# Cluster attention and spatial gating: more MLP buffers, weight splitting on other engines, sums on PE, and new plan constants

## The chip, the cores and the metric

One core of a Trainium2 chip runs the whole kernel. The metric is device time in microseconds (us) of one execution; three runs of the kernel before gave a median of 691.05 (690.49 to 691.19). The engines are PE (matrix products; its loading of weights is shown as PEld), DVE (vector), ACT (activation functions and scaled copies), POOL (a further elementwise engine) and SP, whose queue only issues DMA. Each engine works through its own queue in order.

## The reference

Inputs are q, k and v of 4 batches, 8 heads, 768 positions and 64 dimensions, 16 centroids a head, and the weights of an MLP. Cut to its core:

```python
q_assign = argmax(q_n @ c_n)            # nearest centroid, by cosine
k_assign = argmax(k_n @ c_n)
mask   = q_assign[..., :, None] == k_assign[..., None, :]
scores = where(mask, q @ k.T / sqrt(64), -1e9)
attn   = exp(scores - max(scores)); attn /= sum(attn) + 1e-9
x      = attn @ v                       # heads side by side: 768 x 512
h      = relu(x @ w_in)                 # 512 -> 1024
u, v   = h[..., :512], h[..., 512:]
v_n    = (v - mean(v)) / sqrt(var(v) + 1e-6)
v_s    = w_spatial @ v_n + b_spatial    # over the 768 positions
out    = (u * v_s) @ w_out              # 512 -> 512
```

## The kernel before

**Numbers.** Every fp32 operand of a matrix product is held as two fp16 parts: a high part (a scaled copy, usually on ACT) and a low part (what the rounding left, a scaled difference on DVE or a plain difference on POOL). Products are then three: high times high, high times low, low times high.

**Attention.** A step is a pair of heads; there are 16 (four batches of four pairs), numbered n. `prep(n)` loads q and k and v, splits them, finds the nearest centroids with small products (L553 to L555) and a one-hot encoding on DVE (L566 to L578), and writes these rows beside the head's 64 rows, so that a product over 81 rows yields the masked score. It also makes the sum of v over all positions for rows that meet no key, which goes as two more rows into `mean`. For pairs 0 to 3 that sum is twelve fp16 products with a matrix of ones on PE (L613, L614); for pairs 4 to 15 (`short`) it is a reduction of the raw v on DVE (L621) and two small fp32 products (L622). `shifts(n)` computes each row's maximum: products on PE (L662) and maxima on DVE (L669). `attend(n)` goes over two heads and six tiles of 128 keys each: scores on PE (L713, L715), exp on ACT (L719), high part on ACT (L721), low part on POOL (L722), value products on PE (L727). Then DVE divides by the row's sum, and ACT and POOL split the result x (L750, L751), which a transposing DMA brings into `xT`.

**MLP.** `mlp(b)` runs per batch on six tiles of 128 positions, beside the attention of later batches; the last batch's MLP runs when all attention is done. All its long products are line L771. `v_tile` projects and ACT evicts into `v32` (L792, two buffers, `MV_BUFS`); DVE takes mean and variance; two tiles are normalised together (L811), split on DVE and POOL (L812, L813). `u_tile` projects u (L822). `s_tile` makes the spatial product with `wsp`, DVE adds the bias and multiplies by u (L832), DVE and POOL split it (L833, L834), and a transposing DMA brings it into `gT` (two buffers). `p_tile` makes the output product with `wou`, ACT evicts it into `o32` (L842, one buffer), and ACT's queue issues the store (L843).

**Weights.** `weights` loads each piece and splits it in `lows`: high part on ACT (L461), low part on DVE (L462). `w_in` is split early. `w_spatial` (twelve pieces of 128 x 384, raw buffers `wraw`, two of them) and then `w_out` (eight pieces, three more DVE steps each, L477 to L479) come later, at times given by `WL_AT` and `WL_GAP`. Loads go through SP's queue.

**Order.** All of this is written as operations with an engine, a planned duration, what they come after, and a key. `Plan.run` is a list scheduler: it plays the operations against a model of the engines and, for each engine that comes free, emits the ready operation of the smallest key; for operations of attention the key is added to a due time (`due`, from `DUE_0`, `DUE`, `DUE_M`), for others to the time at which they became ready. So a constant or a planned duration changes the order of instructions on every engine, not the instructions. Buffers of a ring are reused in turn, and the hardware waits follow from the data.

Of the kernel before, what the change touches and what calls it, by code (L numbers as in the profile page):

```python
# [7 lines left out]
F32 = mybir.dt.float32  # L8
F16 = mybir.dt.float16
U32 = mybir.dt.uint32  # L10
AF = mybir.ActivationFunctionType
ALU = mybir.AluOpType
AX = mybir.AxisListType
PSUM = bass.MemoryType.PSUM

P = 128

QK_SCALE = 2.0 ** 5
# [19 lines left out]

R_OH, R_SH, R_E, R_END = 64, 80, 81, 83
P32_BUFS = 3  # L40
DUE_0 = 43.04
DUE = 25.06
DUE_PREP = -1.8
DUE_MAX = -0.66
DUE_M = 31.24
DUE_W = 1.2
PT_BUFS = 4
HQ_BUFS = 4
V_BUFS = 2
MV_BUFS = 2  # L50
U_BUFS = 4
MM = 6
W_KEY = 7.7
WL_KEY = 0.91
WL_AT = 183.98
WL_GAP = 3.25
W_AT = 28.34
W_GAP = 5.52
PREP_KEY = 2.81
AV_KEY = 1.09  # L60
K_SC = -2.4
K_MX = -2.81
K_MAX = -0.27

TBL = 0.14
K_SH = -3.11
K_EXP = 0.71
K_HI = -1.78
K_LO = 2.77
K_RC = -1.64  # L70
K_XD = 3.66
K_X = -1.98
K_VT = -3.58
# [63 lines left out]
class Plan:  # L137
# [12 lines left out]
    def op(self, eng, cost, fn, after=(), use=(), new=(), claim=(), key=0.0, at=0.0, dma=None, turn=False, cols=0, alt=None, due=None):  # L150
        o = Op()
        o.due = self.due if due is None else due
        o.eng, o.cost, o.fn, o.key, o.at, o.dma, o.turn, o.cols, o.alt = eng, cost, fn, key, at, dma, turn, cols, alt
        o.after = [a for a in after if a is not None]
        o.new, o.claim, o.order = list(new), list(claim), []
        o.outs, o.end, o.seq = [], None, len(self.ops)
        for t in list(use) + o.new + o.claim:
            t.users.append(o)
        self.ops.append(o)
        return o  # L160
# [115 lines left out]
def kernel(  # L276
# [24 lines left out]
    V, A, T, G_ = nc.vector, nc.scalar, nc.tensor, nc.gpsimd  # L301
# [5 lines left out]
    moe = ctx.enter_context(tc.tile_pool(name="moe", bufs=2))  # L307
# [4 lines left out]
    op = plan.op  # L312
    R = plan.ring
# [54 lines left out]
    r_y = R(sm, "y", [P, 2], F32, 2)  # L368
    r_y2 = R(sm, "y2", [P, 2], F32, 2)
    r_v32 = R(moe, "v32", [P, DF], F32, MV_BUFS)  # L370
    r_o32 = R(moe, "o32", [P, DM], F32, 1)
    r_u32 = R(moe, "u32", [P, DF], F32, U_BUFS)
    r_ghl = R(moe, "ghl", [P, 2, DF], F16, 1)
    r_gT = R(moe, "gT", [P, 2 * NDT, P], F16, 2)
# [28 lines left out]
    def fill():  # L403
# [27 lines left out]
    o = op("PE", 0.3, lambda: T.transpose(out=ct.t[:, 0:P], in_=scratch.t[:, 0:2 * D], identity=idt()), after=[o, ld_i], use=[scratch], new=[ct], key=KC)  # L431
# [20 lines left out]
    def weights(jobs, at, gap, key, raws, tops, on, after=()):  # L452
        ends = []
        for m, (src, dst, n, lg, wide, cell) in enumerate(jobs):
            raw = raws.new()
            sc = 2.0 ** lg
            t0 = at + gap * m

            def lows(x, ld, n=n, dst=dst, sc=sc, raw=raw, cell=cell, use=()):

                h = op("ACT", 0.2 + 0.00085 * n, lambda: A.activation(out=dst()[:, 0, :], in_=x(), func=AF.Copy, scale=sc), after=ld, use=use, key=key)  # L461
                lo = op("DVE", (0.05 if n > 384 else 0.4) + 0.00125 * n, lambda: V.scalar_tensor_tensor(out=dst()[:, 1, :], in0=x(), scalar=sc, in1=dst()[:, 0, :], op0=ALU.mult, op1=ALU.subtract), after=[h], use=use, key=key)  # L462
                w_ops.setdefault(cell, []).extend([h, lo])
                ends.append(lo)

            if not wide:
                ld = move(on, lambda q, raw=raw, src=src, n=n: q.dma_start(out=raw.t[:, :n], in_=src), new=[raw], dma=1.1, at=t0, key=2, after=after)
                lows(lambda raw=raw, n=n: raw.t[:, :n], [ld], use=[raw])
                continue

            top = tops.new()
            ld = move(on, lambda q, raw=raw, src=src, n=n: q.dma_start(out=raw.t[:, :2 * n].bitcast(U32), in_=src.bitcast(U32)), new=[raw], dma=0.0058 * n, at=t0, key=2, after=after)

            def words(raw, n, k):
# [41 lines left out]
    def prep(n):  # L516
        plan.due = due(n, DUE_PREP) if n else None
        b, p = divmod(n, NPR)
        X = pair[n] = {}
        hq, lo, vh, mw = r_hq.new(), r_lo.new(), r_vhl.new(), r_mean.new()  # L520
        X.update(hq=hq, lo=lo, vhl=vh, mean=mw)
        KP = PREP_KEY if n else KP0
        KV = PREP_KEY + 3.0
        raw, vraw = r_raw.new(), r_vraw.new()
# [5 lines left out]
        his, los = [], []  # L530
        for h, ld in enumerate(raws):
            his.append(op("ACT", 0.83, lambda h=h: A.activation(out=hq.t[:, 0, h, :], in_=raw.t[:, h, :], func=AF.Copy, scale=QK_SCALE), after=[ld], use=[raw] + ([hq] if h else []), new=[] if h else [hq], key=KP))  # L532
        for h, ld in enumerate(raws):
            if n == 1:
                o = op("ACT", 0.83, lambda h=h: A.activation(out=raw.t[:, h, :], in_=raw.t[:, h, :], func=AF.Copy, scale=QK_SCALE), after=[his[h]], use=[raw], key=KP)
                los.append(op("POOL", 1.7, lambda h=h: G_.tensor_tensor(out=lo.t[:, h, :], in0=raw.t[:, h, :], in1=hq.t[:, 0, h, :], op=ALU.subtract), after=[o], use=[raw, hq] + ([lo] if h else []), new=[] if h else [lo], key=KP))
                continue
            los.append(op("DVE", 1.4 if n else 0.96, lambda h=h: V.scalar_tensor_tensor(out=lo.t[:, h, :], in0=raw.t[:, h, :], scalar=QK_SCALE, in1=hq.t[:, 0, h, :], op0=ALU.mult, op1=ALU.subtract), after=[his[h]], use=[raw, hq] + ([lo] if h else []), new=[] if h else [lo], key=KP))  # L538
        if n == 0:
            qa0 = [op("ACT", 0.75, lambda x=x: A.copy(out=hq.t[0:D, x], in_=hq.t[D:P, 0]), after=his, use=[hq], key=KP) for x in (1, 2)]  # L540
        else:
            qa0 = [sp(lambda: nc.sync.dma_start(out=hq.t[0:D, 1:3], in_=hq.t[D:P, 0].unsqueeze(1).broadcast_to([D, 2, 2, S])), 1.8, after=his, use=[hq], key=KP)]
        qa1 = sp(lambda: nc.sync.dma_start(out=hq.t[D:P, 2], in_=lo.t[D:P]), 0.9, after=los, use=[hq, lo], key=KP)
# [69 lines left out]
                T.matmul(out=o[:, :, 0:D + 1], lhsT=ones, rhs=vh.t[:, t, :, 0:D + 1], start=(t == 0), stop=False, skip_group_check=True)  # L613
                T.matmul(out=o[:, :, 0:D], lhsT=ones, rhs=vh.t[:, t, :, D + 2:], start=False, stop=(t == NT - 1), skip_group_check=True)  # L614

        short = n >= NPR
        m = D if short else D + 1
        unit = MEAN_UNIT * (V_SCALE if short else 1.0)
        if short:
            vs = r_vs.new()  # L620
            o = op("DVE", 0.9, lambda: V.tensor_reduce(out=vs.t, in_=vraw.t.rearrange("p t c -> p c t"), axis=AX.X, op=ALU.add), after=[ldv], use=[vraw], new=[vs], key=KV)  # L621
            o = op("PE", 0.4, lambda: T.matmul(out=sv.t[0:2, 0:2 * (D + 2)].rearrange("p (h d) -> p h d", h=2)[:, :, 0:D], lhsT=one32, rhs=vs.t.rearrange("p (h d) -> p h d", h=2), start=True, stop=True), after=[o, c_wh], use=[vs], new=[sv], cols=512, key=KV)  # L622
        else:
            o = op("PE", 0.75, sums, after=[o_vh, o_vl, c_wt], use=[vh], new=[sv], cols=1548, key=KV)
# [136 lines left out]
    def mlp(b):  # L761
# [75 lines left out]
        def p_tile(t, tr, pos):  # L837
            gT = gTs[t]
            o32 = r_o32.new()
            acc, o = acc_group(3 * NDT, lambda: [(gT.t[:, gi * NDT + k, :], held["wou"][:, wi, k, :]) for gi, wi in terms for k in range(NDT)], [tr] + w_ops["wou"], pos, ())  # L840
            gT.users.append(o)
            o = op("ACT", 0.57, lambda: A.activation(out=o32.t, in_=acc.t, func=AF.Copy, scale=2.0 ** -(G_LOG + WOUT_LOG)), after=[o], use=[acc], new=[o32], key=-0.7)  # L842
            op("ACT", 0.06, lambda: A.dma_start(out=out[b, t * P:(t + 1) * P, :], in_=o32.t), after=[o], use=[o32], dma=0.8, key=0)  # L843

        u_ops = {}
        for k, t in enumerate(range(0, NT, 2)):
# [67 lines left out]
```

## Time and profile before

| what | us |
|---|---|
| median of three runs | 691.05 |
| the profiled execution, its own time | 694.26 |
| its span, first to last instruction | 692.5 |
| PE busy | 637.5 |
| DVE, ACT, POOL busy | 482.0, 437.7, 435.3 |

The profile comes from one execution; its span is what the rows below divide up, and its own time is 1.8 us more. "Busy" of PE counts the pipelined products with their ends, so that one product of 512 columns shows 379 ns, though they follow each other every 216 (336 of them took 72.53 us at the end). The granted clock is PE's clock as the throttle allowed it, 1.00 at full speed; its mean was 0.985. A row of a group ends with its count, its busy time and the mean of one in ns, and then the idle time of the engine just before and what ended it.

### The profile page before, as it was taken

What the parts mean: (1) busy time and instruction counts of PE and PEld (TensorE: products, weight loads), DVE (VectorE), ACT (ScalarE), POOL (GpSimd) and SP (SyncE); (2) the same over time, 40 slices, a digit from 0 to 9 for tenths busy, and PEclk for the clock granted to TensorE, in tenths of its full rate; (3) what the DMA queues carried; (4) which work ended last, traced back from release to release, by engine and by line L of the source; (5) the groups of instructions that cost most, each with busy time, mean ns of one, the idle gap of its engine ahead of it and who ended that gap; (6) DMA issues with size and microseconds to landing.
All of it is one profiled execution on the core that took longest, in us unless ns stands there. A gap on an engine that the chain in (4) does not pass through costs nothing.

```text
span 692.5 us, 16725 instructions
## 1 busy us (share of the span) xinstructions
PE 637.5 (92%) x6757; PEld 379.0 (55%) x6757; DVE 482.0 (70%) x940; ACT 437.7 (63%) x685; POOL 435.3 (63%) x305
## 2 busy tenths in 40 slices
PE   2978889999998999988799899999999999999996
PEld 1456566666555655555445556556655655544442
DVE  6999989998969889999754877558485821215210
ACT  5686889998848756678443966667673957412111
POOL 2485778998949667677363976767665966703210
PEclk9998999999999799999999999999999999999999
DMA  5567665574634467442831536262510113140223
GB/s 165 147 154 213 147 107 142 137 168 116 138 110 82 97 165 167 109 116 60 189 61 36 150 74 137 61 152 50 120 34 1 37 28 70 32 115 0 31 61 92
DMA packets 106515, 70.49 MB, mean 102 GB/s; under 512 B 90379, under 2 KB 93126, under 8 KB 106438
## 3 DMA queue, kind: packets, MB, share of 16 engines
q1 hardware_dynamic: 102694, 62.74, 40.4%
q10 hardware_dynamic: 3744, 6.69, 2.7%
q8 instruction: 53, 0.87, 0.5%
q14 instruction: 24, 0.20, 0.1%
HBM read 27.63 MB, written 6.29 MB: 49 GB/s over the span
## 4 chain that ended last, share of the span: by engine, by line
PE 60%; DVE 20%; ACT 9%; issue 5%; DMA 4%; POOL 2%; POOLq 0%; SPq 0%; ACTq 0%; DVEq 0%
PE acc L771 35%; PE acc L727 9%; DVE nm L669 8%; PE acc L662 6%; PE sc L713 5%; PE sc L715 5%; ACT p L719 4%; ACT pt L721 3%; DVE lo L538 2%; POOL pt L722 2%; DMA out_dram<-o 2%; DMA gT<-ghl 1%; ACT hq L532 1%; DVE vhl L606 1%; DVE acc L568 1%
## 5 line engine op out<-in xcount | busy, mean ns | idle before, releaser
L722 POOL TENSOR_TENSOR pt<-p,pt 128x768 f16<-128x768 f32 x192 | 329.7, 1736 | 103.1 <-ACT pt L721 50.6
L719 ACT ACTIVATE p<-sc,plog 128x768 f32<-128x768 f32 x192 | 168.9, 898 | 58.4 <-PE sc L715 53.8
L669 DVE TENSOR_REDUCE nm<-acc 128x1 f32<-128x512 f32 (+1 forms) x288 | 179.8, 683 | 12.4 <-PE acc L662 12.0
L721 ACT CAST pt<-p 128x768 f16<-128x768 f32 x192 | 155.6, 828 | 12.9 <-PE acc L727 11.1
L727 PE MATMUL acc<-vhl,pt 128*128 128x65 f16 (+1 forms) x3456 | 139.2, 196 | 7.6 <-POOL pt L722 6.9
L727 PEld LDWEIGHTS <-pt 128*128 128x128 f16 x3456 | 129.1, 99 | 30.3 <-POOL pt L722 10.1
L771 PE MATMUL acc<-win,xT 128*128 128x512 f16 x576 | 130.0, 379 | 0.0
L662 PE MATMUL acc<-hq 80*128 80x256 f16 (+1 forms) x384 | 101.1, 339 | 20.7 <-DVE nm L669 10.1
L713 PE MATMUL sc<-hq,lo 128*128 128x512 f16 (+1 forms) x384 | 95.7, 331 | 6.3 <-ACT p L719 6.1
L715 PE MATMUL sc<-hq 81*128 81x512 f16 (+1 forms) x384 | 96.0, 331 | 1.0 <-DMA hq<-sht 1.0
L771 PE MATMUL acc<-vn,wsp 128*128 128x512 f16 x432 | 96.8, 379 | 0.0
L771 PEld LDWEIGHTS <-xT 128*128 128x128 f16 x576 | 54.9, 98 | 63.2 <-issue 0.7
L771 PEld LDWEIGHTS <-wsp 128*128 128x128 f16 x432 | 41.8, 98 | 48.9 <-issue 0.2
L834 POOL TENSOR_TENSOR ghl<-u,ghl 128x512 f16<-128x512 f32 x24 | 27.7, 1156 | 64.0 <-DVE ghl L833 49.2
L832 DVE SCALAR_TENSOR_TENSOR u<-acc,bsp,u 128x512 f32<-128x512 f32 x24 | 17.9, 747 | 71.5 <-PE acc L771 71.5
L771 PE MATMUL acc<-wou,gT 128*128 128x512 f16 x288 | 65.6, 379 | 1.7 <-DMA gT<-ghl 1.7
L662 PEld LDWEIGHTS <-hq 80*128 80x128 f16 x384 | 35.3, 99 | 43.2 <-issue 25.1
L538 DVE SCALAR_TENSOR_TENSOR lo<-raw,hq 128x768 f16<-128x768 f32 x30 | 44.9, 1505 | 12.4 <-ACT hq L532 12.0
L713 PEld LDWEIGHTS <-lo 128*128 128x128 f16 x384 | 34.1, 98 | 34.9 <-issue 20.8
L715 PEld LDWEIGHTS <-hq 81*128 81x128 f16 x384 | 37.9, 99 | 27.7 <-issue 2.7
L842 ACT ACTIVATE o<-acc 128x512 f32<-128x512 f32 x24 | 14.3, 597 | 57.0 <-PE acc L771 41.2
L771 PEld LDWEIGHTS <-gT 128*128 128x128 f16 x288 | 27.7, 98 | 33.8 <-DMA gT<-ghl 2.2
(111 smaller groups left out, 628.5 us busy)
## 6 DMA issues: line engine op xcount, KB each, us to landing
raw<-in_kqT_dram SPq DMA_DIRECT2D x15, 768.0 KB
vraw<-in_vp_dram SPq DMA_DIRECT2D x16, 384.0 KB
out_dram<-o ACTq DMA_DIRECT2D x24, 256.0 KB
hq<-hq SPq DMA_DIRECT2D x15, 384.0 KB
vn<-in_w_in_dram SPq DMA_DIRECT2D x8, 512.0 KB
hq<-lo SPq DMA_DIRECT2D x16, 192.0 KB
lo<-hq SPq DMA_DIRECT2D x16, 192.0 KB
wraw<-in_wsT_dram SPq DMA_DIRECT2D x12, 192.0 KB
```

Of the source, the lines that this page charges most:

```text
L538: los.append(op("DVE", 1.4 if n else 0.96, lambda h=h: V.scalar_tensor_tensor(out=lo.t[:, h, :], in0=raw.t[:, h, :], scalar=QK_SCALE, in1= ...
L662: T.matmul(out=acc.t[:, c:c + cs.stop - cs.start], lhsT=hq.t[0:R_SH, 1, h, t * P:(t + 1) * P], rhs=hq.t[0:R_SH, 0, h, cs], start=c == 0, s ...
L669: V.tensor_reduce(out=nm.t[:, t, k:k + 1] if n == 1 else nm.t[:, t:t + n, k], in_=src, axis=AX.X, op=ALU.max, negate=True)
L713: T.matmul(out=sc.t[:, cs], lhsT=lo.t[:, h, ks], rhs=hq.t[:, 2, h, cs], start=True, stop=False)
L715: T.matmul(out=sc.t[:, cs], lhsT=hq.t[0:R_E, 0, h, ks], rhs=hq.t[0:R_E, 1, h, cs], start=False, stop=True)
L719: o = op("ACT", 0.9, lambda sc=sc, p32=p32: A.activation(out=p32.t, in_=sc.t[:, 0:S], func=AF.Exp, bias=plog, scale=SC_UNIT), after=[o, m_ ...
L721: o = op("ACT", 0.83, lambda pt=pt, p32=p32: A.copy(out=pt.t[:, 0, :], in_=p32.t), after=[o], use=[p32], new=[pt], key=K_HI)
L722: o = op("POOL", 1.72, lambda pt=pt, p32=p32: G_.tensor_tensor(out=pt.t[:, 1, :], in0=p32.t, in1=pt.t[:, 0, :], op=ALU.subtract), after=[o ...
L727: T.matmul(out=av.t[:, t * (D + 1):t * (D + 1) + w], lhsT=lhsT, rhs=rhs, skip_group_check=True, **f)
L771: T.matmul(out=acc.t, lhsT=lr[m][0], rhs=lr[m][1], start=(m == 0), stop=(m == n - 1))
L832: o = op("DVE", 0.72, lambda: V.scalar_tensor_tensor(out=u32.t, in0=acc.t, scalar=bsp[:, t:t + 1], in1=u32.t, op0=ALU.add, op1=ALU.mult), ...
L834: l = op("POOL", 1.2, lambda: G_.tensor_tensor(out=ghl.t[:, 1, :], in0=u32.t, in1=ghl.t[:, 0, :], op=ALU.subtract), after=[h], use=[u32, g ...
```

## The change

It alters buffers, places of work, and constants of the plan:

- `MV_BUFS` goes from 2 to 3, and `o32` from one buffer to two.
- The low parts of the twelve pieces of `w_spatial` (not `wide`) are no longer one operation on DVE. ACT scales the raw piece in place, and POOL subtracts the high part from it. `w_in` and `w_out` stay as they were.
- `short` begins at pair 8 instead of 4: pairs 4 to 7 get the twelve products of `sums` in place of the reduction and the two fp32 products, and 65 columns instead of 64 in the steps behind.
- The plan's durations for some operations change (a low part of q and k 1.4 to 1.45, the two copies at the start 0.75 to 1.47, the reduction 0.9 to 1.45, a store 0.8 to 3.0).
- Due times and keys change.

```diff
-DUE_0 = 43.04
-DUE = 25.06
+DUE_0 = 41.15
+DUE = 25.12
...
-DUE_W = 1.2
+DUE_W = 1.54
...
-MV_BUFS = 2
+MV_BUFS = 3
...
-W_KEY = 7.7
-WL_KEY = 0.91
-WL_AT = 183.98
-WL_GAP = 3.25
-W_AT = 28.34
-W_GAP = 5.52
-PREP_KEY = 2.81
-AV_KEY = 1.09
-K_SC = -2.4
-K_MX = -2.81
-K_MAX = -0.27
+W_KEY = 8.65
+WL_KEY = -0.42
+WL_AT = 179.17
+WL_GAP = 3.09
+W_AT = 27.22
+W_GAP = 5.44
+PREP_KEY = 2.91
+AV_KEY = 1.12
+K_SC = -2.1
+K_MX = -2.58
+K_MAX = -0.28
...
-K_SH = -3.11
-K_EXP = 0.71
-K_HI = -1.78
-K_LO = 2.77
-K_RC = -1.64
-K_XD = 3.66
-K_X = -1.98
-K_VT = -3.58
-K_G = -9.5
+K_SH = -2.76
+K_EXP = 0.63
+K_HI = -3.85
+K_LO = 5.38
+K_RC = -0.08
+K_XD = 4.23
+K_X = -1.89
+K_VT = -3.15
+K_G = -15.43
...
-    r_o32 = R(moe, "o32", [P, DM], F32, 1)
+    r_o32 = R(moe, "o32", [P, DM], F32, 2)
...
                 h = op("ACT", 0.2 + 0.00085 * n, lambda: A.activation(out=dst()[:, 0, :], in_=x(), func=AF.Copy, scale=sc), after=ld, use=use, key=key)
-                lo = op("DVE", (0.05 if n > 384 else 0.4) + 0.00125 * n, lambda: V.scalar_tensor_tensor(out=dst()[:, 1, :], in0=x(), scalar=sc, in1=dst()[:, 0, :], op0=ALU.mult, op1=ALU.subtract), after=[h], use=use, key=key)
+                if not wide:
+                    o = op("ACT", 0.2 + 0.00085 * n, lambda: A.activation(out=x(), in_=x(), func=AF.Copy, scale=sc), after=[h], use=use, key=key)
+                    lo = op("POOL", 0.1 + 0.0021 * n, lambda: G_.tensor_tensor(out=dst()[:, 1, :], in0=x(), in1=dst()[:, 0, :], op=ALU.subtract), after=[o], use=use, key=key)
+                else:
+                    lo = op("DVE", (0.05 if n > 384 else 0.4) + 0.00125 * n, lambda: V.scalar_tensor_tensor(out=dst()[:, 1, :], in0=x(), scalar=sc, in1=dst()[:, 0, :], op0=ALU.mult, op1=ALU.subtract), after=[h], use=use, key=key)
...
-            los.append(op("DVE", 1.4 if n else 0.96, ...
+            los.append(op("DVE", 1.45 if n else 0.96, ...
...
-            qa0 = [op("ACT", 0.75, ...
+            qa0 = [op("ACT", 1.47, ...
...
-        short = n >= NPR
+        short = n >= 2 * NPR
...
-            o = op("DVE", 0.9, lambda: V.tensor_reduce(out=vs.t, ...
+            o = op("DVE", 1.45, lambda: V.tensor_reduce(out=vs.t, ...
...
-            op("ACT", 0.06, lambda: A.dma_start(out=out[b, t * P:(t + 1) * P, :], in_=o32.t), after=[o], use=[o32], dma=0.8, key=0)
+            op("ACT", 0.06, lambda: A.dma_start(out=out[b, t * P:(t + 1) * P, :], in_=o32.t), after=[o], use=[o32], dma=3.0, key=0)
```

More of the change, by code (lines that the diff above doesn't have):

```diff
@@ L457, in weights, with lows @@
             t0 = at + gap * m
-            def lows(x, ld, n=n, dst=dst, sc=sc, raw=raw, cell=cell, use=()):
+            def lows(x, ld, n=n, wide=wide, dst=dst, sc=sc, raw=raw, cell=cell, use=()):
                 h = op("ACT", 0.2 + 0.00085 * n, lambda: A.activation(out=dst()[:, 0, :], in_=x(), func=AF.Copy, scale=sc), after=ld, use=use, key=key)
-                lo = op("DVE", (0.05 if n > 384 else 0.4) + 0.00125 * n, lambda: V.scalar_tensor_tensor(out=dst()[:, 1, :], in0=x(), scalar=sc, in1=dst()[:, 0, :], op0=ALU.mult, op1=ALU.subtract), after=[h], use=use, key=key)
+                if not wide:
[3 more added lines that the diff above has]
+                    lo = op("DVE", (0.05 if n > 384 else 0.4) + 0.00125 * n, lambda: V.scalar_tensor_tensor(out=dst()[:, 1, :], in0=x(), scalar=sc, in1=dst()[:, 0, :], op0=ALU.mult, op1=ALU.subtract), after=[h], use=use, key=key)
                 w_ops.setdefault(cell, []).extend([h, lo])
@@ L537, in prep @@
                 continue
-            los.append(op("DVE", 1.4 if n else 0.96, lambda h=h: V.scalar_tensor_tensor(out=lo.t[:, h, :], in0=raw.t[:, h, :], scalar=QK_SCALE, in1=hq.t[:, 0, h, :], op0=ALU.mult, op1=ALU.subtract), after=[his[h]], use=[raw, hq] + ([lo] if h else []), new=[] if h else [lo], key=KP))
+            los.append(op("DVE", 1.45 if n else 0.96, lambda h=h: V.scalar_tensor_tensor(out=lo.t[:, h, :], in0=raw.t[:, h, :], scalar=QK_SCALE, in1=hq.t[:, 0, h, :], op0=ALU.mult, op1=ALU.subtract), after=[his[h]], use=[raw, hq] + ([lo] if h else []), new=[] if h else [lo], key=KP))
         if n == 0:
-            qa0 = [op("ACT", 0.75, lambda x=x: A.copy(out=hq.t[0:D, x], in_=hq.t[D:P, 0]), after=his, use=[hq], key=KP) for x in (1, 2)]
+            qa0 = [op("ACT", 1.47, lambda x=x: A.copy(out=hq.t[0:D, x], in_=hq.t[D:P, 0]), after=his, use=[hq], key=KP) for x in (1, 2)]
         else:
@@ L620, in prep @@
             vs = r_vs.new()
-            o = op("DVE", 0.9, lambda: V.tensor_reduce(out=vs.t, in_=vraw.t.rearrange("p t c -> p c t"), axis=AX.X, op=ALU.add), after=[ldv], use=[vraw], new=[vs], key=KV)
+            o = op("DVE", 1.45, lambda: V.tensor_reduce(out=vs.t, in_=vraw.t.rearrange("p t c -> p c t"), axis=AX.X, op=ALU.add), after=[ldv], use=[vraw], new=[vs], key=KV)
             o = op("PE", 0.4, lambda: T.matmul(out=sv.t[0:2, 0:2 * (D + 2)].rearrange("p (h d) -> p h d", h=2)[:, :, 0:D], lhsT=one32, rhs=vs.t.rearrange("p (h d) -> p h d", h=2), start=True, stop=True), after=[o, c_wh], use=[vs], new=[sv], cols=512, key=KV)
```

## The prediction

> **What bounds the kernel now.** I read the page first (TensorE, PE, is busy 92%), then the busy time by stretches of the span, to see in which stretch PE is not the bound.
>
> ```profile
> span 692.5 us, 16725 instructions
> PE 637.5 (92%) x6757; PEld 379.0 (55%) x6757; DVE 482.0 (70%) x940; ACT 437.7 (63%) x685; POOL 435.3 (63%) x305
> ...
> core 0: us, PE busy (x) PEld busy (x) DVE busy (x) ACT busy (x) POOL busy (x), PEclk, DMA share, GB/s
> 100.00:180.00 80.00, 74.43 (x1138) 51.25 (x1135) 77.26 (x142) 76.01 (x121) 74.06 (x46) 1.00 0.63 144
> 180.00:212.00 32.00, 32.00 (x268) 17.09 (x265) 24.41 (x57) 19.56 (x34) 20.01 (x15) 1.00 0.43 110
> 212.00:246.00 34.00, 29.01 (x387) 19.45 (x386) 29.96 (x47) 27.02 (x45) 28.50 (x18) 0.85 0.53 110
> 246.00:296.00 50.00, 49.92 (x528) 29.19 (x526) 48.46 (x81) 31.30 (x50) 31.34 (x21) 1.00 0.59 146
> 296.00:346.00 50.00, 41.44 (x503) 25.93 (x501) 43.52 (x73) 34.24 (x54) 30.49 (x20) 1.00 0.49 115
> 346.00:400.00 54.00, 51.79 (x481) 29.08 (x481) 33.91 (x74) 32.16 (x52) 35.68 (x26) 1.00 0.33 80
> 400.00:680.00 280.00, 278.74 (x2543) 155.30 (x2542) 135.17 (x278) 142.55 (x220) 156.72 (x113) 1.00 0.30 64
> ```
>
> From 400 us on PE has 1.26 us idle in 280: there nothing but PE's own work counts, and whatever PE could not do earlier is added at the end. Before 180 us (first batch, no MLP work yet) DVE, ACT and POOL are all nearly full: 77.26, 76.01 and 74.06 of 80. Between, two stretches stand out: PE is idle 34.00 - 29.01 = 4.99 us in 212 to 246 and 50.00 - 41.44 = 8.56 us in 296 to 346. An idle microsecond of PE there is a microsecond of the span if other PE work is ready to fill it. I looked up what PE waited for in both, in the waits by stretch (the first two rows from 212 to 246, the last from 296 to 346), and followed the chain of waits.
>
> ```profile
> PE acc L662 <- DVE nm L669: 2.8, 3, 2.1
> PE acc L727 <- POOL pt L722: 1.3, 2, 1.0
> ...
> PE acc L662 <- ACT o L842: 3.4, 2, 1.8
> ...
> 330.34 4.57 DMA out_dram<-o
> ...
> 335.63 6.43 DMA out_dram<-o
> ```
>
> The second stretch: L842 writes the MLP's result tile to its only buffer, and cannot until the store of the tile before has landed. ACT is a queue in order, so exps and casts stand behind it; the maxima on PE (L662) wait too.
>
> The first stretch: PE did no MLP work between 212 and 246, since the spatial product needs the last piece of the spatial weights. These rows (groups by shape, then timelines of ACT, DVE and PE) show how that piece came so late.
>
> ```profile
> L462 DVE SCALAR_TENSOR_TENSOR wsp<-wraw,wsp 128x384 f16<-128x384 f32 x12 | 11.3, 938 | 2.0 <-ACT wsp L461 2.0
> L461 ACT ACTIVATE wsp<-wraw 128x384 f16<-128x384 f32 x12 | 6.2, 518 | 0.8 <-DMA wraw<-in_wsT_dram 0.7
> ...
> 227.38 0.52 ACT L461 ACTIVATE wsp<-wraw 128x384 f16<-128x384 f32 x1
> ...
> 238.96 0.64 DVE L462 SCALAR_TENSOR_TENSOR wsp<-wraw,wsp 128x384 f16<-128x384 f32 x1
> ...
> 244.47 1.52 DVE L462 SCALAR_TENSOR_TENSOR wsp<-wraw,wsp 128x384 f16<-128x384 f32 x1 [1.70 <-ACT wsp L461]
> ...
> 245.85 1.46 PE L771 MATMUL acc<-vn,wsp 128*128 128x512 f16 x6
> ```
>
> High parts done by 227.90 waited until 238.96 on DVE; only that freed the two raw buffers for the last load, whose low part ran at 244.47, and PE began the spatial product at 245.85.
>
> **The change, part by part.**
>
> A. *Two result buffers.* The two waits of PE for L842, 3.4 us together, go. The store is 4.57 and 6.43 us, and a third tile can still meet the first store, so the gain lies between 0 and the idle that the stretch holds, 8.56. I take 3.4, the row that names the wait. The longer store in the plan (0.8 to 3.0) issues nothing more; it only shifts order. DMA's share there is 0.49, which covers it; uncovered it costs one store wait, 4.57.
>
> B. *Spatial low parts off DVE.* DVE loses 12 instructions, 11.3 us. ACT gains 12 in-place scalings of L461's shape, 12 x 0.518 = 6.2 us, and POOL 12 subtractions whose nearest row is the same shape of L751:
>
> ```profile
> L751 POOL TENSOR_TENSOR xhl<-xn,xhl 128x384 f16<-128x384 f32 x32 | 32.7, 1023 | 5.2 <-ACT xhl L750 5.1
> ...
> 219.58 10.28 POOL L722 TENSOR_TENSOR pt<-p,pt 128x768 f16<-128x768 f32 x6
> 222.00:232.00 10.00, 9.27 (x73) 5.68 (x73) 8.61 (x14) 6.50 (x10) 7.86 (x5) 0.50 0.81 130
> ```
>
> 12 x 1.023 = 12.3 us. From 180 to 246 ACT has 66.00 - 46.58 = 19.42 us free and POOL 66.00 - 48.51 = 17.49, so both fit in total, but not in 219.58 to 229.86, where POOL ran six subtractions without a break: there one low part delays an attention subtraction by 1.02. Each job also becomes longer, 0.52 + 0.52 + 1.02 against 0.52 + 0.54 to 1.95; against that it no longer queues 11 us behind DVE's maxima, and its raw buffer and SP's next load come earlier (the loads are also asked for 4.8 us earlier at first, 6.6 at last: 183.98 to 179.17, gaps 3.25 to 3.09). PE then has spatial products to put into the idle 4.99 us. From 222 to 232 it also ran at a granted clock of 0.50, so 9.27 busy did the work of 4.64. Bounds: no gain, and 4.99 + 4.64 = 9.6. I take 4.99 less one POOL low part in the way, 4.0, and nothing for the clock, since POOL's unbroken row shows that attention could not have gone faster there.
>
> [...]
>
> ```profile
> L538 DVE SCALAR_TENSOR_TENSOR lo<-raw,hq x30: 908/1436/2402, 7.0 to 454.9; 128x768 f16<-128x768 f32 x30
> L462 DVE SCALAR_TENSOR_TENSOR wsp<-wraw,wsp x12: 535/556/1953, 195.0 to 244.5; 128x384 f16<-128x384 f32 x12
> ```
>
> [...]
>
> [...]
>
> C. *Sums of pairs 4 to 7 on PE.* DVE loses four reductions, at 114 to 184 us. PE loses two fp32 matmuls a pair and gains twelve. The rows are the grouped reduction, one matmul pair, and first and last of the twelve for pair 3:
>
> ```profile
> L621 DVE TENSOR_REDUCE vs<-vraw 128x128 f32<-128x768 f32 x12 | 18.0, 1498 | 0.8 <-DMA vraw<-in_vp_dram 0.8
> 100.00:180.00 80.00, 4.54 (x3) 1.00 0.63 144
> 188.30 0.38 PE L622 MATMUL acc<-vs,one 128*2 128x128 f32 x2
> 95.78 0.22 PE L613 MATMUL acc<-vhl,ones 128*128 128x130 f16 x1
> ...
> 96.42 0.22 PE L614 MATMUL acc<-vhl,ones 128*128 128x128 f16 x1
> ...
> L601 ACT ACTIVATE vhl<-vraw 128x768 f16<-128x768 f32 x16 | 13.4, 839 | 0.0
> ...
> L606 DVE SCALAR_TENSOR_TENSOR vhl<-vraw,vhl 128x768 f16<-128x768 f32 x14 | 20.5, 1462 | 0.2
> ```
>
> Three of the four, 4.54 us, lie in 100 to 180, where DVE is fullest. But ACT is only 80.00 - 76.01 = 3.99 us from full there, so the gain is 0 to 3.99; I take 1.3, a third, as three engines share that bound. On PE twelve take 96.42 + 0.22 - 95.78 = 0.86 against 0.38: 0.48 more a pair. Three are covered by PE's 5.57 us idle in 100 to 180; the fourth meets a full PE (32.00 of 32.00): loss 0.5, at worst 1.9. The sums now wait for the low parts of v instead of running beside them, about 1.3 us later (0.84 + 1.46 + 0.86 against 1.50 + 0.38, by the means of L601, L606 and the rows above); pairs are prepared ahead, which hides it.
>
> D. *Three v buffers.* In 180 to 212 ACT waits for POOL's normalised low parts before it can empty a v tile:
>
> ```profile
> ACT v L792 <- POOL vn L813: 6.9, 2, 4.1
> ```
>
> PE is full in that stretch, so I cost it at nothing; if ACT then starves PE later it is worth one such wait, 4.1, and a loss has no mechanism except SBUF space, which nothing else uses.
>
> E. *Keys, due times, planned durations.* They remove no instruction; they reorder every queue, the first batch included. What they do I can't read from a trace: bounds -3.5 to +3.5, an estimate from the idle time that PE still has after 346 us and that no part above touches (2.21 to 400, 1.26 after): order could take it away or double it. I take 0.
>
> Sum: -3.4 - 4.0 - 1.3 + 0.5 = -8.2. The profiled execution took 694.26 us with a span of 692.5; it becomes 686.1 with a span of 684.3. The median of the runs is 691.05, 3.2 below the profiled one; the same difference gives **682.9 us**, 1.2% faster.
>
> **Rivals.**
>
> 1. *The fill moves its wait* (686.9). Spatial products come earlier, but their output has two transposed buffers, which only the output product empties, and that needs weights whose work on DVE runs on until about this row:
>
> ```profile
> 325.63 5.34 PE L771 MATMUL acc<-wou,gT 128*128 128x512 f16 x24
> ```
>
> [...] Then B is 0 and PE's idle time reappears after 246: 691.05 - 3.4 - 1.3 + 0.5 = 686.9. Against it: that work can start as soon as the raw buffers are free, which is earlier.
>
> 2. *Both engines come free* (675.9). B at 9.6 with the clock kept, and two thirds of C (2.7): 691.05 - 3.4 - 9.6 - 2.7 + 0.5 = 675.9. [...] Against: POOL's unbroken row.
>
> 3. *Slower: POOL's order* (695.2). The key of attention's low parts goes from 2.77 to 5.38, so x's low parts (1.023 each, two a pair) and weights pass ahead of them, and PE's value products wait. Over the eight pairs before PE is full that is at most 16 x 1.02 = 16.4; with twelve of the sixteen it is 12.3 - 8.2 = 4.1 slower, and it turns from gain to loss at eight, 8.2. For it: POOL 74.06 of 80 from 100 to 180. Against: four buffers stand between POOL and PE, and PE waited for POOL only 1.3 us from 212 to 246.
>
> 4. *Nothing* (690.5). The third tile of a run still meets the first store, C is taken by ACT, B by rival 1: what is left is 0.5.
>
> **How the numbers follow.** Forecast 0.46, rival 1 0.19, rival 2 0.13, rival 3 0.14, rival 4 0.08. A difference of 0.2%, 1.4 us, is about what measurement can tell. The forecast's own range is 678 to 688 (E at either end, and A or C half as large). The whole range is 675 to 693: it takes in rivals 1, 2 and 4 and the near part of 3. Rival 1 is 4 us faster than before but may shrink under the bound, so faster is 0.46 + 0.16 + 0.13 = 0.75; within 0.2% 0.03 of rival 1 and most of 4, 0.10; slower 0.15.
>
> **What would show it.** A: no wait of L842 for the store, and PE idle in the output products below 5 us instead of 8.56. B: POOL's new rows near 1.0 us, ACT's near 0.52, spatial products begun before 235 us instead of 245.85, and no stretch of clock 0.5 after 212. C: DVE below 76 of 80 in 100 to 180 and attention of the first batch over 1 us earlier. Wrong it is if PE's idle time before 400 us stays, whichever engine it then waits for; rival 3 would show as waits of L727 for L722 above the 6.9 us that the whole trace has now:
>
> ```profile
> PE acc L727 <- POOL pt L722: 6.9, 13, 1.0
> ```

## The result, and the profile after

| | before | after |
|---|---|---|
| median of seven runs, us | 691.19 | 687.41 |
| lowest to highest | 690.29 to 695.73 | 686.26 to 689.48 |
| the profiled execution's own time | 694.26 | 686.60 |
| its span | 692.5 | 684.8 |

The ratio is 0.9937, interval 0.9917 to 0.9958: faster by 0.63%, half of what was forecast. Mind the third row: the profiled execution of before lies 3.07 us above its median, that of after 0.81 below. The spans differ by 7.7 us, the medians by 3.78.

The page of after, its first lines:

```profile
span 684.8 us, 16820 instructions
PE 637.6 (93%) x6797; PEld 379.7 (55%) x6797; DVE 468.4 (68%) x924; ACT 442.5 (65%) x697; POOL 444.8 (65%) x317
```

Busy time of after by the same stretches as before (us, then PE, PEld, DVE, ACT, POOL, the granted clock, DMA's share and GB/s):

```profile
100.00:180.00 80.00, 76.08 (x1178) 55.02 (x1176) 71.37 (x137) 76.84 (x123) 74.48 (x46) 0.98 0.66 143
180.00:212.00 32.00, 30.19 (x319) 17.45 (x318) 26.35 (x47) 23.80 (x44) 26.32 (x22) 1.00 0.43 121
212.00:246.00 34.00, 30.52 (x343) 18.48 (x339) 28.65 (x52) 26.12 (x46) 27.71 (x22) 0.85 0.50 127
246.00:296.00 50.00, 47.20 (x509) 27.88 (x506) 47.04 (x84) 32.41 (x52) 33.49 (x21) 1.00 0.67 145
296.00:346.00 50.00, 48.90 (x548) 29.81 (x547) 34.58 (x65) 37.75 (x60) 36.32 (x24) 1.00 0.49 97
346.00:400.00 54.00, 53.17 (x585) 31.18 (x583) 41.00 (x84) 35.54 (x59) 34.27 (x26) 1.00 0.35 89
400.00:680.00 280.00, 276.28 (x2405) 151.18 (x2406) 129.77 (x263) 133.59 (x205) 152.33 (x109) 1.00 0.32 64
```

PE is busy 637.6 us where it was 637.5, so the whole difference of the two spans is idle time of PE. It did not fall everywhere. PE's idle time, before and after: 5.57 and 3.92 (100 to 180), 0 and 1.81 (180 to 212), 4.99 and 3.48 (212 to 246), 0.08 and 2.80 (246 to 296), 8.56 and 1.10 (296 to 346), 2.21 and 0.83 (346 to 400), 1.26 and 3.72 (400 to 680). One stretch holds most of the fall, the one of the store waits; three got worse.

What PE waited for from 296 to 346 (us in total, times, longest):

```profile
PE acc L775 <- ACT o L846: 0.6, 1, 0.6
PE acc L666 <- DVE ohx L582: 0.5, 1, 0.5
```

And one of ACT's waits there:

```profile
ACT o L846 <- DMA out_dram<-o: 3.3, 1, 3.3
```

Busy time in a stretch inside 212 to 246:

```profile
219.50:229.70 10.20, 9.48 (x59) 5.22 (x59) 9.09 (x18) 5.85 (x11) 9.18 (x8) 0.50 0.43 123
```

The timeline of PE where the spatial products begin:

```profile
240.63 1.67 PE L775 MATMUL acc<-vn,wsp 128*128 128x512 f16 x7
```

Of PE's 3.4 us behind the store 0.6 are left, though ACT still waited once for a store, 3.3 us. The 10.2 us at a clock of 0.50 are still there, and the spatial products began only 5.2 us earlier (240.63 for 245.85). The new operations cost what was estimated. Groups by shape (busy, mean of one in ns, idle time before and its causes):

```profile
L464 POOL TENSOR_TENSOR wsp<-wraw,wsp 128x384 f16<-128x384 f32 x12 | 12.4, 1033 | 2.6 <-ACT wraw L463 2.6
...
L461 ACT ACTIVATE wsp<-wraw 128x384 f16<-128x384 f32 x12 | 6.2, 520 | 4.3 <-DMA wraw<-in_wsT_dram 4.3
```

Minimum, median and maximum of POOL's new line:

```profile
L464 POOL TENSOR_TENSOR wsp<-wraw,wsp x12: 910/916/1628, 187.8 to 238.9; 128x384 f16<-128x384 f32 x12
```

The row of L461 shows that ACT now waited 4.3 us for the loads of the pieces. All of these waits lie in 180 to 212, though, and are not what made the last piece late. Its load was issued at 231.60, right behind POOL's subtraction of the tenth piece (230.37 to 231.28), which frees the raw buffer. ACT took it among its other work at 237.19, without waiting for the load, and POOL waited for ACT's second scaling (timelines of ACT and POOL):

```profile
237.19 0.51 ACT L461 ACTIVATE wsp<-wraw 128x384 f16<-128x384 f32 x1
...
238.92 0.92 POOL L464 TENSOR_TENSOR wsp<-wraw,wsp 128x384 f16<-128x384 f32 x1 [1.62 <-ACT wraw L463]
```

### The profile page after: what moved, and what is told of

It is laid out like the page before. It is cut to its first block, busy times and chain, and to the rows that moved or that the text cites. A ratio compares the mean times of both kernels' runs of the same rounds, so it can differ in the third digit from the quotient of the medians.

```text
span 684.8 us, 16820 instructions
## 1 busy us (share of the span) xinstructions
PE 637.6 (93%) x6797; PEld 379.7 (55%) x6797; DVE 468.4 (68%) x924; ACT 442.5 (65%) x697; POOL 444.8 (65%) x317
## 4 chain that ended last, share of the span: by engine, by line
PE 60%; DVE 21%; ACT 9%; issue 4%; DMA 3%; POOL 2%; SPq 0%; ACTq 0%; POOLq 0%; DVEq 0%
PE acc L775 34%; PE acc L731 9%; DVE nm L673 8%; PE acc L666 6%; PE sc L717 5%; PE sc L719 5%; ACT p L723 3%; ACT pt L725 2%; POOL pt L726 2%; DVE lo L542 2%; DMA raw<-in_kqT_dram 1%; DVE vhl L610 1%; DVE wou L466 1%; DVE acc L573 1%; ACT hq L536 1%
## 5 line engine op out<-in xcount | busy, mean ns | idle before, releaser
L726 POOL TENSOR_TENSOR pt<-p,pt 128x768 f16<-128x768 f32 x192 | 325.9, 1715 | 85.0 <-ACT pt L725 52.1
L731 PE MATMUL acc<-vhl,pt 128*128 128x65 f16 (+1 forms) x3456 | 136.9, 194 | 10.7 <-POOL pt L726 10.4
L731 PEld LDWEIGHTS <-pt 128*128 128x128 f16 x3456 | 126.6, 98 | 32.4 <-POOL pt L726 13.2
L838 POOL TENSOR_TENSOR ghl<-u,ghl 128x512 f16<-128x512 f32 x24 | 29.9, 1244 | 64.9 <-DVE ghl L837 61.7
L846 ACT ACTIVATE o<-acc 128x512 f32<-128x512 f32 x24 | 14.3, 597 | 61.2 <-PE acc L775 57.9
L817 POOL TENSOR_TENSOR vn<-v,vn 128x512 f16<-128x512 f32 x24 | 29.6, 1246 | 27.4 <-DVE vn L816 24.5
```

The lines of the kernel that those rows point to most:

```text
L726: o = op("POOL", 1.72, lambda pt=pt, p32=p32: G_.tensor_tensor(out=pt.t[:, 1, :], in0=p32.t, in1=pt.t[:, 0, :], op=ALU.subtract), after=[o ...
L731: T.matmul(out=av.t[:, t * (D + 1):t * (D + 1) + w], lhsT=lhsT, rhs=rhs, skip_group_check=True, **f)
L817: l = op("POOL", 1.3, lambda t=t, v=v: G_.tensor_tensor(out=vn[:, 1, t, :], in0=v.t, in1=vn[:, 0, t, :], op=ALU.subtract), after=[h], use= ...
L838: l = op("POOL", 1.2, lambda: G_.tensor_tensor(out=ghl.t[:, 1, :], in0=u32.t, in1=ghl.t[:, 0, :], op=ALU.subtract), after=[h], use=[u32, g ...
```

## The experiments

The question was which part carries the gain. Changing any part makes the planner choose another order on every engine, so most runs below fix the order: the plan is made first, from the kernel as it was, and its finished order is then issued with one part exchanged. All other instructions stay where they were. Ratios are to the kernel before, timed beside each group of four (its medians 691.35, 692.34 and 692.43).

### Two result buffers on the old order

```diff
 # the plan is made with one result buffer; its order is issued with
-    r_o32 = R(moe, "o32", [P, DM], F32, 1)
+    r_o32 = R(moe, "o32", [P, DM], F32, 2)
```

> Edit: the order of instructions on every engine is kept exactly as the kernel before has it (its plan is made first, with one result buffer, and then issued); only o32 has two buffers. Nothing is left out. The prediction (A, 3.4 us): ratio 0.995, the waits of PE for L842 gone, PE idle in 296 to 346 about 5 us instead of 8.56. Rival 'nothing' (the third tile meets the first store): 0.999 to 1.000, with a wait of ACT for the store left. Rival 'order' (what was gained came from the new keys alone): 1.000, because PE's idle time reappears before 400 us.

Measured: 1.0002 (0.9988 to 1.0015). Busy time of this kernel from 296 to 346:

```profile
296.00:346.00 50.00, 45.19 (x515) 27.97 (x514) 46.89 (x75) 37.51 (x58) 32.98 (x22) 0.97 0.49 115
```

Its longest waits of ACT in that stretch:

```profile
ACT p L731 <- PE sc L727: 5.8, 6, 1.7
ACT o L854 <- PE acc L783: 4.5, 3, 2.3
```

And of PE:

```profile
PE acc L674 <- DVE ohx L590: 1.7, 2, 1.6
```

No wait there names the store any more, and PE is idle 4.81 us, as A had said (about 5). Yet the time did not change. This kernel's profiled execution took 691.49 us, its median is 691.45: it shows a typical execution, and that of before does not. Since the medians agree, the 2.8 us between the two spans (692.5 and 689.7) can't be put down to the buffer. How long the store wait is in a typical execution of before no trace here shows; only one execution of it was traced, and in that one a store took 6.43 us. One rival stays open: the mean granted clock is 0.986 over this kernel's twelve executions and 0.989 over the seventeen of before beside them. The difference, 0.0026 of 691, is 1.8 us of PE's work at full speed (an estimate), so a gain of that size may be hidden behind the clock.

### Spatial low parts on ACT and POOL, on the old order

```diff
-                lo = op("DVE", ..., lambda: V.scalar_tensor_tensor(...), after=[h], ...)
+                lo = op("DVE", ..., lambda: (A.activation(out=x(), in_=x(), func=AF.Copy, scale=sc), G_.tensor_tensor(out=dst()[:, 1, :], in0=x(), in1=dst()[:, 0, :], op=ALU.subtract)), after=[h], ...)
```

> Edit: the order of before is kept; where the plan had the low part of a spatial piece on DVE, ACT's in-place scaling and POOL's subtraction are issued instead. One result buffer, two v buffers, old keys. The prediction (B, 4.0 us): ratio 0.994, spatial products begun before 240 us instead of 245.85. [...] Slower is possible if POOL's low parts in 212 to 246 delay attention: up to 5 x 1.02 us, 1.007.

Measured: 1.0119 (1.0095 to 1.0142), slower by more than any theory had. Busy time of this kernel from 212 to 246:

```profile
212.00:246.00 34.00, 28.19 (x384) 19.09 (x382) 25.99 (x45) 28.56 (x48) 30.54 (x22) 0.85 0.46 94
```

Its timeline of PE at the first spatial product:

```profile
245.41 0.81 PE L783 MATMUL acc<-vn,wsp 128*128 128x512 f16 x3
```

Its waits of PE from 180 to 246:

```profile
PE acc L739 <- POOL pt L734: 2.5, 3, 1.1
PE acc L674 <- DVE nm L681: 1.6, 2, 1.4
```

DVE was freed (25.99 of 34 busy for 29.96) and PE got no work from it: the products began at 245.41, 0.44 earlier. The order still asked for the pieces where DVE would have had time for them. PE's idle time there rose from 4.99 to 5.81, and its waits for POOL in the stretch are now the longest. These rows account for about 1 us. A second place lies far behind them. Up to 485 us this kernel's exps fall 2.6 us behind those of the run above, which has the same order; by 552 us they are 6.2 behind. Between, PE waited once for the maxima, and then ran 6.80 us without a pause at half clock (timeline and busy time of this kernel):

```profile
502.69 0.38 PE L674 MATMUL acc<-hq 80*128 80x512 f16 x1 [1.67 <-DVE nm L681]
...
503.40:510.20 6.80, 6.80 (x37) 3.63 (x36) 4.94 (x9) 4.20 (x7) 2.99 (x3) 0.50 0.05 15
```

So of the 6.1 us between these two traced executions (697.62 and 691.49), some 3.4 were lost at that clock (an estimate, half of 6.80). Why DVE was late there was not followed.

### All the structure but the sums, on the old order

```diff
 # order of before; then
+    o32: 2 buffers, v32: 3 buffers, spatial low parts as in the run above
```

> Edit: the order of before is kept; two result buffers, three v buffers, and the spatial low parts on ACT and POOL, all at once. The sums of pairs 4 to 7 stay on DVE. The prediction (A and B, 7.4 us): ratio 0.989. Rival 1 (A alone counts): 0.995. Rival 'order': 1.000.

Measured: 1.0080 (1.0051 to 1.0110). The buffers take back perhaps a third of what the low parts cost; the intervals touch.

### The new order with the work put back

```diff
 # order of the changed kernel; in place of ACT's scaling and POOL's subtraction
+                    lo = op(..., lambda: V.scalar_tensor_tensor(...), ...)
 # behind the low part of v that DVE makes (pairs 2 to 15)
+                if n < 2 * NPR:
+                    ...
+                    V.tensor_reduce(out=vs4[0], in_=vraw.t.rearrange("p t c -> p c t"), axis=AX.X, op=ALU.add)
 # for pairs 4 to 7, in place of the twelve products
+                T.matmul(..., lhsT=one32, rhs=vs4[0]..., start=True, stop=True)
```

> Edit: the order of the changed kernel is kept on every engine, but the work is put back as it was before: the spatial low parts on DVE (issued where POOL's were), and the sums of pairs 4 to 7 as a reduction on DVE (issued right behind the low part of v) and two fp32 products. The two result and three v buffers stay, since this order needs them. The prediction (A alone, the new order costing nothing): 0.995. Rival 1 says the same, 0.995, and the changed kernel no better. If B and C carry the gain, this run loses what they brought: near 1.000 or above, with DVE fuller than 77 of 80 us in 100 to 180. Rival 'order': as fast as the changed kernel, 0.994 or less.

Measured: 1.0070 (1.0058 to 1.0082). The text above is wrong on two points. A run below shows that this order also runs with one result buffer. And the work is not quite as it was before: `n < 2 * NPR` holds for pairs 2 and 3 as well, whose sums stay on PE, so DVE makes two reductions that nothing reads. In the run with the sums on DVE, below, these two cost 2.3 us; without them this run would stand near 1.004 (an estimate, 2.3 of 691 taken off). That is still no faster than before, so the new order alone is not what made the kernel faster.

### The changed kernel, for comparison

> The changed kernel itself, as the measure for the three runs beside it. All theories: 0.994 (0.992 to 0.996, as timed before).

Measured: 0.9914 (0.9891 to 0.9938). The next three runs were timed beside it.

### The new order with one result buffer

```diff
 # order of the changed kernel, issued with
-    r_o32 = R(moe, "o32", [P, DM], F32, 2)
+    r_o32 = R(moe, "o32", [P, DM], F32, 1)
```

> Edit: the changed kernel's order kept on every engine, with one result buffer instead of two. The prediction (A worth 3.4 us): 0.999. After the run of two buffers on the old order, which gained nothing (1.000), I expect the buffer to matter only where the order puts results close together: 0.995 to 0.997, with waits of ACT for the store again.

Measured: 0.9909 (0.9886 to 0.9931), the same as with two. The waits came back, and cost nothing (waits of this kernel over the whole span):

```profile
ACT o L858 <- DMA out_dram<-o: 14.3, 5, 3.6
```

### The new order with spatial low parts on DVE

```diff
 # order of the changed kernel; ACT's in-place scaling left out, POOL's place issues
+                    lo = op(..., lambda: V.scalar_tensor_tensor(...), ...)
```

> Edit: the changed kernel's order kept, with the spatial low parts back on DVE, issued where POOL's were planned; ACT's in-place scaling is left out, as it isn't needed. The prediction (B worth 4.0 us): 1.000. Theory 'the order was made for it' (a part costs when it doesn't fit the plan, whichever way it is moved): slower than the changed kernel by some us although DVE then works no more than before, 0.996 to 1.000. Rival 1 (B worth nothing): 0.994.

Measured: 0.9929 (0.9904 to 0.9953), against 0.9914 a loss of 0.15%, about 1 us, inside both intervals. B is worth at most little.

### The new order with the sums of pairs 4 to 7 on DVE

```diff
 # order of the changed kernel; behind the low part of v that DVE makes (pairs 2 to 15)
+                if n < 2 * NPR:
+                    ...
+                    V.tensor_reduce(out=vs4[0], in_=vraw.t.rearrange("p t c -> p c t"), axis=AX.X, op=ALU.add)
 # for pairs 4 to 7, in place of the twelve products
+                T.matmul(..., lhsT=one32, rhs=vs4[0]..., start=True, stop=True)
```

> Edit: the changed kernel's order kept, with the sums of pairs 4 to 7 back as a reduction on DVE (right behind the low part of v) and two fp32 products. The prediction (C worth 1.3 - 0.5): 0.995. If DVE was the bound of 100 to 180 us: up to three reductions, 4.5 us, 1.000. The run with B and C both put back lost 1.3% against the changed kernel, so this one and the one with DVE low parts should lose some 9 us together if they add up.

Measured: 1.0036 (1.0016 to 1.0057): the gain is gone, 1.2% or 8.4 us of it by the ratios (0.0122 of 691), 7.26 us by the two medians. But the edit puts six reductions on DVE, not four: those of pairs 2 and 3, whose sums stay on PE, are made and never read. DVE has 930 instructions for 924. All six by minimum, median and maximum, then the second and the third:

```profile
L628 DVE TENSOR_REDUCE vs<-vraw x6: 1466/1478/1501, 63.2 to 211.0; 128x128 f32<-128x768 f32 x6
...
96.38 1.47 DVE L628 TENSOR_REDUCE vs<-vraw 128x128 f32<-128x768 f32 x1
...
123.76 1.49 DVE L628 TENSOR_REDUCE vs<-vraw 128x128 f32<-128x768 f32 x1
```

The third, at 123.76, is the first that belongs to pairs 4 to 7. The exps, twelve a pair, tell the two groups apart. Timeline of ACT in the changed kernel of the same group: the eleventh and twelfth exp, the 39th, the 96th (pair 7's last), and the last two:

```profile
51.55 1.69 ACT L723 ACTIVATE p<-sc,plog 128x768 f32<-128x768 f32 x2
...
119.25 0.90 ACT L723 ACTIVATE p<-sc,plog 128x768 f32<-128x768 f32 x1
...
272.81 0.90 ACT L723 ACTIVATE p<-sc,plog 128x768 f32<-128x768 f32 x1 [0.28 <-POOL pt L726]
...
584.71 1.69 ACT L723 ACTIVATE p<-sc,plog 128x768 f32<-128x768 f32 x2 [0.50 <-PE sc L719]
```

The same exps of this kernel:

```profile
52.05 1.69 ACT L747 ACTIVATE p<-sc,plog 128x768 f32<-128x768 f32 x2
...
122.03 0.88 ACT L747 ACTIVATE p<-sc,plog 128x768 f32<-128x768 f32 x1
...
279.52 0.91 ACT L747 ACTIVATE p<-sc,plog 128x768 f32<-128x768 f32 x1 [0.28 <-POOL pt L750]
...
591.33 1.69 ACT L747 ACTIVATE p<-sc,plog 128x768 f32<-128x768 f32 x2 [0.50 <-PE sc L743]
```

This kernel is 0.50 us behind at the eleventh exp and 2.78 at the 39th, when only the two unread reductions have run: 2.3 us are theirs. It is 6.71 behind at pair 7's last exp and 6.62 at the last of all, so from 280 us to the end the two run alike. For the four reductions of pairs 4 to 7 that leaves 3.8 us between these two traces (6.62 - 2.78), 5.0 by the medians (7.26 - 2.3) and 6.1 by the ratios (8.4 - 2.3): some 4 to 6 us, where the four take 5.9 us of DVE. They are still the part that weighs most. A run with these four alone was not made.

Busy time of the changed kernel in the first 180 us:

```profile
0.00:100.00 100.00, 74.68 (x932) 48.35 (x932) 89.77 (x198) 75.97 (x116) 59.90 (x53) 0.97 0.58 157
100.00:180.00 80.00, 75.36 (x1171) 54.45 (x1168) 73.38 (x136) 75.55 (x121) 72.85 (x46) 0.98 0.64 140
```

Busy time of this kernel, with the reductions:

```profile
0.00:100.00 100.00, 71.78 (x896) 47.05 (x897) 89.11 (x195) 73.10 (x111) 58.15 (x53) 0.96 0.57 153
100.00:180.00 80.00, 71.81 (x1094) 49.38 (x1093) 73.26 (x134) 72.73 (x115) 68.97 (x43) 0.99 0.60 139
```

ACT's two longest waits in 100 to 180 with the reductions:

```profile
ACT xhl L778 <- DVE xn L776: 2.9, 2, 1.5
ACT wl L660 <- DVE w L659: 1.4, 2, 0.8
```

DVE is no busier (162.37 for 163.15), since it gets less done; PE, ACT and POOL all lose, PE in part because the edit takes products from it. ACT, which in the changed kernel is nearly full here, stands still for DVE's results.

### The sums alone, with the old constants

```diff
-        short = n >= NPR
+        short = n >= 2 * NPR
```

> Edit: the kernel before, with the sums of pairs 4 to 7 on PE and nothing else; the plan is made anew with the old keys, due times and durations. If the sums by themselves carry the gain (they lost 1.2% when put back in the new order): 0.990 to 0.994. If they need the new constants: 0.998 to 1.003. The prediction (C worth 1.3 - 0.5): 0.999.

Measured: 1.0075 (1.0052 to 1.0099), slower. The same work moved off DVE, planned anew with the old constants, loses. Attention does come earlier at first: the 66th exp starts at 174.10 us, for 176.23 in before. Its busy time by stretches:

```profile
100.00:180.00 80.00, 75.00 (x1200) 54.10 (x1197) 71.80 (x137) 77.32 (x123) 76.39 (x47) 1.00 0.63 145
...
212.00:246.00 34.00, 27.57 (x401) 18.78 (x399) 33.73 (x60) 28.85 (x47) 28.77 (x18) 0.95 0.40 94
246.00:296.00 50.00, 47.29 (x452) 26.98 (x452) 45.21 (x72) 26.52 (x44) 25.37 (x17) 0.97 0.49 119
296.00:346.00 50.00, 43.85 (x495) 26.28 (x493) 39.56 (x67) 34.27 (x52) 32.28 (x21) 0.97 0.57 129
```

The first batch does become denser (DVE 71.80, ACT 77.32). Then PE is idle 6.43, 2.71 and 6.15 us, 15.3 in all where before had 13.6: the old constants leave DVE full to 33.73 of 34 between 212 and 246.

### The sums undone, planned anew with the new constants

```diff
-        short = n >= 2 * NPR
+        short = n >= NPR
```

> Edit: the changed kernel with the sums of pairs 4 to 7 as a reduction on DVE and two fp32 products again, the plan made anew with the new constants, so that it knows of the reductions. If the loss of 1.2% in the fixed order was DVE's work itself: 0.999 to 1.004. If it was only the place where the reductions were put: 0.992 to 0.995, as the changed kernel.

Measured: 1.0057 (1.0035 to 1.0079), slower than either theory had. With four reductions, and a plan that knows of them, the gain is gone as well. How much of this is DVE's work and how much the order the run does not tell, for the plan made anew orders much else differently: its 18th exp starts at 75.94 us, 3.3 later than in the changed kernel of the group before (72.67), and its first reduction only at 105.01.

### The new constants alone

```diff
 # all keys, due times and planned durations of the change; buffers, low parts and sums as before
```

> Edit: the kernel before (one result buffer, two v buffers, spatial low parts and sums on DVE) with all new keys, due times and planned durations, the plan made anew. The prediction (E worth nothing): 1.000. Theory 'order' (the constants are worth something by themselves): 0.994 to 0.998. Theory 'made for each other' (constants of another structure fit this one badly): 1.003 to 1.010.

Measured: 1.0127 (1.0108 to 1.0147), the slowest of all, though not told from the low parts on the old order (1.0119). Busy time in its worst stretch:

```profile
246.00:296.00 50.00, 43.62 (x385) 24.52 (x384) 44.91 (x79) 23.63 (x41) 26.26 (x18) 0.83 0.44 109
```

What PE waited for there longest:

```profile
PE acc L775 <- DVE nm L673: 3.9, 2, 3.7
```

And ACT:

```profile
ACT wou L461 <- DVE top L483: 14.1, 6, 4.4
```

DVE still has the spatial low parts and the reductions, and under these constants its work on the output weights keeps ACT waiting 14.1 us; PE is idle 6.38 and at a clock of 0.83.

### Sums of pairs 8 and 9 on PE too

```diff
-        short = n >= 2 * NPR
+        short = n >= 10
```

> Edit: the changed kernel with the sums of pairs 8 and 9 on PE too, the plan made anew. If DVE is what holds attention up to about 300 us, two more reductions off it gain 1 to 3 us against the changed kernel: 0.987 to 0.990, with pair 9's exps ending earlier. If PE is the bound there by then, its 0.48 us more a pair shows: 0.992 to 0.995.

Measured: 0.9940 (0.9921 to 0.9960), the same as the changed kernel (0.9937, and 0.9914 in the other group). More sums off DVE bring nothing further.

## Why the prediction was right, and where not

The sign and the range held. The size came out half, and hardly one term stood: A and B, 7.4 of the 8.2 us, gave little or nothing, and C gave more than it was put down for. That the sum fell on the right side, and within the range, is in good part luck. What follows goes by the prediction's own letters.

**The step from the sum to the median** failed first: "The median of the runs is 691.05, 3.2 below the profiled one; the same difference gives **682.9 us**". The sum was -8.2, and the profiled executions do differ by 7.66, which is luck, as the terms show. But the medians differ by 3.78. The execution whose rows were added up was 3 us slower than its kernel usually is, so some of the waits in it belonged to that execution. That the store wait was among them is argued, from the run of two result buffers, not shown.

**A**, -3.4, measured 0.0 on the old order (-0.8 to +1.0 us) and nothing on the new one. PE's waits did go, but for 0.6 us in 296 to 346, though the sign "no wait of L842 for the store" did not come: ACT still waited once, 3.3 us. The waits' worth did not follow: in the new order ACT waits 14.3 us for stores with one buffer, and the kernel is as fast.

**B**, -4.0, measured +8 us on the old order and about -1, not told from 0, on the new. The durations were right (1.033 for 1.023, 0.52). The step "PE then has spatial products to put into the idle 4.99 us" failed: products begun before 235 us were the sign asked for, and they began at 240.63. The last piece was late again, now behind ACT's other work (237.19, for a load issued at 231.60), and the stretch at clock 0.50 stayed. Whether PE at half clock there costs anything, which B took as nothing, was therefore not tested.

**C**, -1.3 + 0.5, was the term that came out larger: some 4 to 6 us in the new order, with the two unread reductions taken off, and a loss of 5 with the old constants. The signs that it had asked for came: DVE is busy 71.37 of 80, and the 48th exp, the last of the first batch, starts 2.5 us earlier (135.31 for 137.85). The step that failed is "I take 1.3, a third, as three engines share that bound". ACT's busy share did not cut the gain to a third: with the reductions back ACT did not stay full, it fell to 72.73 of 80, and its longest waits there are for DVE. Whether the bound itself, 3.99, holds stays open, as 3.8 and 5.0 lie on either side of it. What PE lost by its twelve products can't be read from its totals: 637.5 before and 637.6 after, but 639.4 in another execution of the changed kernel.

**D** was not tried alone. The new order was taken to need the third buffer, which no run tested, so what D is worth stays open.

**E**, taken at 0 with bounds of 3.5, was the worst: the constants alone cost 8.8 us (0.0127 of 692) on the old structure. And that shows what was wrong with the sum as such. Each of A, B, C and E alone costs something or nothing on the old kernel (1.000, 1.012, 1.008, 1.013), and together they gain. The gain is neither in one part alone nor in the order alone. The sums off DVE and constants that fit them are needed at once: the sums without the constants stand at 1.0075, everything but the sums at 1.0057. A and B could be left out of the changed kernel, one at a time, at little or no loss. Whether the old constants, planned anew with all four edits, would do was not tried.

**The rivals.** The time is rival 1's (686.9), but not by its reason: it kept A at 3.4, which measured 0, and C at 1.3. Its picture of B fits better: B is worth little, and 2.80 us of idle time stand in 246 to 296 where there were 0.08. That this is the same idle time moved was not shown. Rival 3 named POOL; PE's waits for it did rise over the whole span of after, and the kernel gained all the same:

```profile
PE acc L731 <- POOL pt L726: 10.4, 17, 1.3
```

**DVE's durations and the clock.** DVE lost 11.3 + 6.0 = 17.3 us of instructions and its busy time fell by 13.6 (482.0 to 468.4), or by 10.0 with another execution of the changed kernel (472.0). So 3.7 to 7.3 us came back, on balance, in instructions that both kernels have. Not all of them became longer: the low part of q and k went from 1436 ns in the median before to 1000. Minimum, median and maximum of its line in after:

```profile
L542 DVE SCALAR_TENSOR_TENSOR lo<-raw,hq x30: 911/1000/2395, 7.1 to 435.1; 128x768 f16<-128x768 f32 x30
```

A small step of the MLP's normalisation became 5.2 us longer in all (groups by shape, of before and then of after):

```profile
L804 DVE TENSOR_SCALAR a<-mv 128x2 f32<-128x2 f32 x12 | 3.7, 306 | 0.4
...
L808 DVE TENSOR_SCALAR a<-mv 128x2 f32<-128x2 f32 x12 | 8.9, 740 | 0.4
```

What changed these durations was not shown. On the clock, PE waits for the maxima close to the slow stretch in both traces (timeline of PE, in before and then in after):

```profile
219.97 0.38 PE L662 MATMUL acc<-hq 80*128 80x256 f16 x2 [2.09 <-DVE nm L669]
...
220.21 0.59 PE L666 MATMUL acc<-hq 80*128 80x256 f16 x2 [2.01 <-DVE nm L673]
```

In before the clock is 0.50 from 222 to 232, in after from 219.50 to 229.70. The length of a wait alone does not settle it: a wait of 1.67 us stands ahead of the 6.80 us at 0.50 in the run of the spatial low parts on the old order, and one of 1.8 us, for L842, lies in 296 to 346 of before, where the clock is 1.00. What lowers the clock was not shown. At 0.50 PE's products take about twice the time: groups of two score products start 0.64 us apart there, and 0.32 to 0.33 apart at 1.00 (timeline of PE in after, the first two rows at 0.50, the others at 1.00):

```profile
223.97 0.84 PE L717 MATMUL sc<-hq,lo 128*128 128x512 f16 x2
224.61 0.84 PE L719 MATMUL sc<-hq 81*128 81x512 f16 x2
...
237.23 0.49 PE L717 MATMUL sc<-hq,lo 128*128 128x512 f16 x2
237.55 0.49 PE L719 MATMUL sc<-hq 81*128 81x512 f16 x2
237.88 0.49 PE L717 MATMUL sc<-hq,lo 128*128 128x512 f16 x2
```

The clock may also hold much of what the slower kernels lost. Over all its runs a kernel's mean granted clock is 0.985 for the changed kernel and 0.986 to 0.989 for before, but 0.979 for the low parts on the old order, 0.978 for the sums put back and 0.977 for the constants alone. The slow stretches show 0.50, so 0.01 less in the mean is 14 us more at half clock (0.01 of 691, twice) and up to 7 us of PE's work, an estimate. Whether the clock is a cause there or only follows PE's waits is not shown. The gain does not come from it, as the changed kernel's clock is no higher than before's. Nor do the 2.3 us of the two unread reductions, as far as the rounded clocks tell: from 0 to 100 and from 100 to 140 us they are 0.97 and 0.96 in the changed kernel and 0.96 and 0.98 with the reductions, which leaves 4.6 and 4.8 us of the 140 not granted.

## What to carry to other kernels

Add up terms only from an execution that is near its kernel's median, or say which part of the sum may belong to that execution alone. Where a planner orders the work, parts don't add: cost a part in the order it will run in, and hold the order fixed to learn what a part is worth. That a second engine is nearly as full as the first says little on what freeing the first brings, since each may be waiting for the other in turns. And count an engine's instructions before reading what an experiment cost: 930 for 924 on DVE were six reductions, where four were meant.

## What the runs showed that was not expected

- Moving 11.3 us of work off DVE made the kernel 1.2% slower when the order stayed (1.0119), and a change of constants alone 1.3% slower (1.0127). A tuned order is worth more here than any single wait in it.
- ACT can wait 14.3 us in all for stores and the time does not change (0.9909 beside 0.9914).
- Executions of one kernel with one fixed order differ more than the 0.2% that the prediction put down as what a measurement can tell: 690.29 to 695.73 for the kernel before. The intervals of the ratios are 0.1 to 0.3% to either side.
